# Loading queries and keys by head pair instead of by row tile, moving the first values to another queue, and building the sine tables later, in a fused attention and gated-convolution kernel

## The chip, the cores and the metric

The kernel runs on one core of a Trainium2 chip. The metric is the device time of one execution in microseconds (us). A "span" is the length of the profiled execution; it is some 2 us shorter than the device time of the same run. A run is called slow when its time is more than 1.5% above the fastest of the same kernel, and only fast runs enter a comparison. The share of full speed that the throttle granted to the matrix engine is called the granted clock.

Five engines appear in the profile: PE (matmuls; PEld is its weight load), ACT (activations, copies), DVE (vector work), POOL and SP (here mostly issuers of transfers). A line such as L381 is a line of the kernel concerned, so the same work has another line number in the kernel before (L376) and after (L381).

## The reference, cut to what matters

```python
# q, k, v: (4 batches, 8 heads, 768 positions, 64), float32
scores = q @ k.T / 8 - slope[h] * distance, kept for the 8 global keys
         and for the 96 positions up to the query; softmax; @ v
x = attention output as (4, 768, 512)
x1, x2, x3 = split(x @ w_proj, 3)              # w_proj: (512, 1536)
conv = irfft(rfft(x2) * rfft(filter_fft))      # along the 768 positions
out  = (x1 * conv * x3) @ w_out                # float32
```

The kernel does the Fourier transforms as matmuls with sine tables, in four batches. A batch passes through: load q and k (float32 in memory, float16 on the chip), transpose them, scores, exps, masks, values, transpose x, projection ("proj"), forward transform, products, inverse transform, gates, output ("out").

Of the kernel before, what the change touches and what calls it, by code (L numbers as in the profile page):

```python
# [9 lines left out]
F32 = mybir.dt.float32  # L10
# [5 lines left out]
P = 128  # L16
# [44 lines left out]
class Plan:  # L61
# [55 lines left out]
    def schedule(self):  # L117
# [27 lines left out]
        dma = [2.0]  # L145
# [4 lines left out]
        while live:  # L150
# [25 lines left out]
            if o.bytes:  # L176
                n, size = o.bytes
                dma[0] = max(dma[0], o.end + 1.8) + n * size / (306e3 if size < 512 else 390e3)
                ready = o.landed = dma[0] + 0.3
# [98 lines left out]
class Fused:  # L278
# [26 lines left out]
    def buffers(self):  # L305
# [5 lines left out]
        self.qn = t("qn", [P, 6, H, D])  # L311
        self.kn = t("kn", [P, 7, H, D])
# [23 lines left out]
        self.ot = [t(f"ot{i}", [P, DM], F32) for i in range(6)]  # L336
# [3 lines left out]
        self.dm = t("dm", [P, 3, 216], F32)  # L340
        self.dg = t("dg", [P, 216], F32)
# [37 lines left out]
    def load_rows(self, what, dst, src, b, t):  # L379

        lo, hi = max(0, self.K0[t] - NG), self.K0[t] + KL  # L381
        self.load("G", dst[P - (hi - lo):P, t, :, 0:self.D],
                  src[b, :, lo:hi, :].rearrange("h p d -> p h d"), [what + (t,)], (8 * (hi - lo), 256),
                  f"load{what}{t}")

    def load_q(self, b, t):
        src = self.q[b, :, P * t:P * t + P, :].rearrange("h p d -> p h d")
        if b == 0:
            st = self.ot[t].rearrange("p (h d) -> p h d", h=self.H)
            self.load("S", st, src, [("ot", t)], (1024, 256), f"q{t}")  # L390
            self.g.op("V", dve(512, 2), lambda e: self.copy(e, self.qn[:, t], st),
                      r=[("ot", t)], w=[("qn", t)], name="cast")
        else:
            self.load("G", self.qn[:, t], src, [("qn", t)], (1024, 256), f"q{t}")

    def load_v(self, b, ts):
        vt, s = self.vn[b % 2], b % 2
        if b < 2 and ts[0] == 0:
            self.g.op("V", 0.2, lambda _: self.nc.vector.memset(vt[:, :, :, self.D:], 1.0),
                      w=[("vn1", s)], name="ones")  # L400
        for t in ts:
            self.load_rows(("vn", s), vt, self.v, b, t)
            if t == 0:
                self.load_global(vt, s, 0, 1)
            elif t == ts[-1]:
                lo = max(1, ts[0])
                self.load_global(vt, s, lo, t + 1 - lo)
# [6 lines left out]
    def load_w(self, o, n):  # L414
        wr = self.w_proj.rearrange("(t p) n -> p t n", p=P)
        self.load("G", self.w[:, :, o:o + n], wr[:, :, o:o + n],
                  [("w", i) for i in range(o // P, (o + n) // P)], (512, 4 * n), f"w{o}")


    def setup(self):  # L420
# [4 lines left out]
        g.op("A", 0.2, lambda _: nc.scalar.activation(self.warm, self.warm, Act.Sin),  # L425
             r=["warm"], w=["warm"], table="sin", bias=-4000)
# [13 lines left out]
        g.op("V", 0.08, lambda _: v.memset(self.kn[0:NG, 0], 0.0), w=[("kn", 0)], bias=-4000)  # L440
# [9 lines left out]
    def tables(self):  # L450

        nc, g, S = self.nc, self.g, self.S
        nf = 2.0 * math.pi / S * (1.0 - 4.0e-7)
        for a in range(5):
            b = g.bank()
            g.op("P", 0.8 if a < 3 else 0.5, lambda _, a=a, b=b: self.angles(a, b.f32()),
                 r=["rows"], acq=[b], bias=-3000, name="angles")
# [4 lines left out]
                w=[("th", a)], bias=-3000)  # L462
            g.op("V", dve(n, 2), lambda _, th=th: nc.vector.tensor_scalar(
                th, th, MAGIC, -float(S), op0=Alu.subtract, op1=Alu.mult), r=[("th", a)],
                w=[("th", a)], bias=-3000)
            g.op("V", dve(n), lambda _, th=th, b=b, n=n: nc.vector.tensor_add(
                th, th, b.f32()[:, 0:n]), use=[b], r=[("th", a)], w=[("th", a)], bias=-3000)
            part = range(0, 2) if a == 3 else range(2, 3)

            def sines(_, a=a, th=th, part=part):  # L470
                if a < 3:
                    o = self.fwd[:, a, 0:4].rearrange("p s r -> p (s r)")
                else:
# [5 lines left out]
                 [("fwd", t, s) for t in part for s in (4, 5)], table="sin", bias=-3000,  # L479
                 name="sines")  # L480
# [34 lines left out]
    def distances(self):  # L515
# [4 lines left out]
        p, v, dm, dg = nc.gpsimd, nc.vector, self.dm, self.dg  # L520

        def first(_):
            for ap, w, base in ((dg, n, NG), (dm[:, 2, n - 48:n], 48, NG + o)):
# [7 lines left out]
            p.affine_select(dm[:, 2, n - 48:n], dm[:, 2, n - 48:n], pattern=[[0, 48]],  # L531
                            base=-NG - o, channel_multiplier=1, compare_op=Alu.is_ge, fill=HUGE)
        g.op("G", 1.8, first, w=["dm"], bias=-2000.0 + 5)

        def second(_):
            v.tensor_copy(dm[:, 0:2], dg[:, None, :].to_broadcast([P, 2, n]))
            v.tensor_copy(dm[:, 2, 0:n - 48], dg[:, 0:n - 48])
            v.memset(dm[0:NG, :, 0:KL], float(NL))
            v.memset(dm[0:NG, :, KL:n], HUGE)
            v.memset(dm[0:NG, 2, n - 48:n], float(NL))  # L540
            v.memset(dm[0:NG, 0, 0:KL], HUGE)
        g.op("V", 1.6, second, r=["dm"], w=["dm"], bias=-100)

        def third(_):
            d0 = dm[0:NG, 0, 0:KL]
            for sgn, off in ((1, 0), (-1, NL - 1)):
                p.affine_select(d0, d0, pattern=[[sgn, KL]], base=off, channel_multiplier=-sgn,
                                compare_op=Alu.is_ge, fill=float(NL))
        g.op("G", 0.65, third, r=["dm"], w=["dm"], bias=-2000.0 + 5)
        for h in range(self.H):  # L550
            g.op("A", act(648), lambda _, h=h: nc.scalar.activation(
                self.mask[:, h], dm.rearrange("p a b -> p (a b)"), Act.Exp, scale=-self.slopes[h]),
                r=["dm"], w=[("mask", h)], table="exp", name="mask",
                after=[x for x in g.ops if x.name == "sines"])
# [46 lines left out]
    def transposes(self, what, t, src, cols):  # L601

        nc, g = self.nc, self.g
        b = g.bank()

        def turn(_):
            for i in range(4):
                nc.tensor.transpose(b.f16()[:, P * i:P * i + P],  # L608
                                    src[:, 2 * i:2 * i + 2, :], self.ident)
        g.op("P", pe(*[128] * 4), turn, acq=[b], r=["ident", (what + "n", t)], name=what)  # L610
        lo = NG if what == "k" else 0
        dst = self.QT[:, :, cols:cols + P] if what == "q" else self.KT[:, :, cols + lo:cols + P]
        g.op("AV", {"A": act(512), "V": dve(512, 2, True)}, lambda e: self.copy(
            e, dst, b.f16()[:, 0:512].rearrange("p (i c) -> p i c", i=4)[:, :, lo:]), use=[b],
            w=[(what.upper() + "T", t)], name=what + "T")
        if what == "k" and t == 0:
            kv = self.KT.rearrange("p i (t c) -> p i t c", t=7)
            g.op("V", dve(224), lambda _: self.copy(
                "V", kv[:, :, :, 0:NG], kv[:, :, 0:1, NG:2 * NG].to_broadcast([P, 4, 7, NG])),
                r=[("KT", 0)], w=["KTg"])  # L620

    def scores(self, hp, gi):
# [15 lines left out]
        qt = range(KL * m0[0] // P, (KL * m0[-1] + self.EW[m0[-1]] - 1) // P + 1)  # L638
        g.op("P", 0.34, run, acq=bs, r=[("QT", t) for t in qt] + [("KT", m) for m in m0] + ["KTg"],
# [4 lines left out]
        for hh in range(2):  # L644
            g.op("A", act(432), lambda _, hh=hh: nc.scalar.activation(  # L645
                eo[:, hh], bs[hh].f32()[:, 0:432].rearrange("p (m w) -> p m w", m=2), Act.Exp,
                scale=self.scale), use=[bs[hh]], w=[("E", hp, gi, hh)], table="exp", name="exp")
        mk = self.mask[:, 2 * hp:2 * hp + 2].rearrange("p h (m w) -> p h m w", m=3)

        def masked(_):  # L650
# [4 lines left out]
            else:  # L655
                nc.vector.tensor_mul(eo, eo, mk[:, :, 0:2] if gi == 0 else mk[:, :, 1:3])  # L656
        g.op("V", dve(864, 2) + (0.068 if gi == 1 else 0), masked,
             r=[("E", hp, gi, 0), ("E", hp, gi, 1), ("mask", 2 * hp), ("mask", 2 * hp + 1)],
# [42 lines left out]
    def transpose_x(self, j, c):  # L701
# [5 lines left out]
        def run(_):  # L707
# [10 lines left out]
            w=[("xT", j, c)], name="xT")  # L718

    def butterfly(self, j):  # L720
        g, h, hs = self.g, self.S // 2, slice(2 * j, 2 * j + 2)
        xT = self.xT
        rs = [("xT", j, c) for c in range(3)]
# [5 lines left out]
    def gate(self, b, j, s):  # L729
        nc, g, h = self.nc, self.g, self.S // 2  # L730
        gt = self.gt[b % 2]
        xs = [("xT", i, c) for i in range(2) for c in ((0, 1) if s == 0 else (1, 2))]
# [18 lines left out]
    def attention(self, b):  # L751
        self.g.batch = (self.PERIOD * (b - 1 + self.SHIFT), self.PERIOD * self.LONG)
        for c in range(3):
            new = ([0, 1, 2], [3, 4], [5])[c]
            for t in new:
                self.transposes("q", t, self.qn[:, t], P * t)
            for t in self.GRP[c]:
                self.transposes("k", t, self.kn[:, t], P * t)
# [133 lines left out]
    def load_first(self):  # L892
        for c in range(3):
            for t in ([0, 1, 2], [3, 4], [5])[c]:
                self.load_q(0, t)
            for t in self.GRP[c]:
                self.load_rows(("kn",), self.kn, self.k, 0, t)
            if c == 0:
                self.distances()
            self.load_v(0, self.GRP[c])  # L900
        wr = self.w_proj.rearrange("(t p) n -> p t n", p=P)
        for o in (0, 256):
            self.load_w(o, 256)
            self.load_w(2 * self.DM + o, 256)
        self.load_w(self.DM, self.DM)
        self.load("G", self.fl, self.filt.rearrange("(t p) n -> p t n", p=P),
                  [("g", 1, j, s) for j in range(4) for s in range(2)], (768, 2048), "filter")

    def load_batch(self, b):
        for t in range(6):  # L910
            self.load_q(b, t)
        for t in range(7):
            self.load_rows(("kn",), self.kn, self.k, b, t)
        self.load_v(b, range(7))

    def graph(self):
# [3 lines left out]
        self.tables()  # L920
        self.load_first()
        self.attention(0)
        g.batch = (0.0, self.PERIOD / 2)
# [53 lines left out]
```

## The kernel before: what the change and the argument touch

The kernel lists its operations with their cost, their reads (`r=`) and their writes (`w=`). A list scheduler then orders them greedily for each engine by estimated times and by a priority that grows with the batch. What it puts out is a fixed order for each engine. Two facts matter later. First, `r=` and `w=` are names inside the scheduler; the waits that the chip carries out are derived from the tiles that the instructions really touch. Second, the scheduler estimates when a transfer lands.

```python
# scheduler: one line of transfers for the whole chip
n, size = o.bytes
dma[0] = max(dma[0], o.end + 1.8) + n * size / (306e3 if size < 512 else 390e3)
ready = o.landed = dma[0] + 0.3
...
key = lambda o: o.batch[0] + o.batch[1] * o.tail / (total[o.batch] or 1.0) + o.bias
# batch 0's loads; load_q(0, t): SP, float32, then a cast; else POOL, which casts on the way
def load_first(self):
    for c in range(3):
        for t in ([0, 1, 2], [3, 4], [5])[c]:
            self.load_q(0, t)                       # 128 positions, 8 heads, rows of 256 bytes
        for t in self.GRP[c]:
            self.load_rows(("kn",), self.kn, self.k, 0, t)
        if c == 0:
            self.distances()                        # masks
        self.load_v(0, self.GRP[c])                 # values, on POOL as well
    ...                                             # then the weights and the filter, on POOL
# a transpose: four 128x128 blocks (head pairs) of one row tile t into one bank, one copy out
nc.tensor.transpose(b.f16()[:, P * i:P * i + P], src[:, 2 * i:2 * i + 2, :], self.ident)
# attention of a batch: chunk by chunk, only the tiles that a chunk needs
self.g.batch = (self.PERIOD * (b - 1 + self.SHIFT), self.PERIOD * self.LONG)   # SHIFT 0, LONG 0.8
for c in range(3):
    for t in ([0, 1, 2], [3, 4], [5])[c]:
        self.transposes("q", t, self.qn[:, t], P * t)
    for t in self.GRP[c]:                            # (0,1), (2,3), (4,5,6)
        self.transposes("k", t, self.kn[:, t], P * t)
    for i in range(4):
        self.scores(i, c)
    ...                                              # values, transpose x, gates
# graph: the sine tables come first, with the highest priority (bias -3000)
self.setup(); self.tables(); self.load_first(); self.attention(0)
```

The softmax here doesn't subtract the row's maximum and nothing guards it: scores larger than these inputs give would overflow.

## Time and profile before

| | before |
|---|---|
| time, median of 3 runs (lowest to highest) | 199.46 us (199.36 to 200.19) |
| span of the profiled run | 198.0 us |
| PE busy | 185.1 us, 93% |
| transfers' packets | 90,933 |
| exps of batch 0, start of the first to start of the last | 20.9 to 32.2 us |
| first output matmul of batch 0, 1, 2; last one of all | 90.9, 128.3, 165.8; 193.7 us |

The page of the kernel before, its first part (busy us, share of the span, instructions) and the lines of its second part for PE and its clock, in 40 slices of 5 us, in tenths:

```profile
PE 185.1 (93%) x1654; PEld 109.7 (55%) x1654; DVE 151.0 (76%) x380; ACT 150.3 (76%) x305; POOL 75.7 (38%) x96
...
PE   7993699989999699999999999999999999999992
...
PEclk9998599999999969999999999999999999999999
```

PE is the engine to watch: it is nearly always busy from 40 us on. It is short of work at 15 to 25 us, and the clock falls to 0.5 there. The queues of the same page (packets, MB, share of the time of 16 DMA engines), and the summary of the chain that ended last:

```profile
q0 software_dynamic: 80912, 12.52, 95.7%
q1 hardware_dynamic: 10000, 8.10, 12.6%
...
PE 72%; DMA 10%; POOL 9%; DVE 4%; issue 2%; ACT 1%; POOLq 0%; ACTq 0%
```

POOL's queue is q0, SP's is q1. The opening, from the chain in order of time (start us, us, what):

```profile
22.84 9.44 DMA w<-in_moe_w_proj_dram
...
32.57 9.87 DMA kn<-in_k_dram
...
43.53 5.20 PE bank L739 x32
```

The program waits for projection weights until 32.3 us and for batch 1's keys until 42.4 us. ACT's timeline of the opening shows the table loaded again, the masks, and the first exps:

```profile
14.54 1.28 ACT L551 ACT_TABLE_LOAD   x1
15.83 5.17 ACT L551 ACTIVATE mask<-dm 128x648 f16<-128x648 f32 x8
20.91 6.80 ACT L645 ACTIVATE E<-bank 128x432 f16<-128x432 f32 x16
```

Two lines of the windows view. Its columns are the window and its length, then busy us and instructions of PE, PEld, DVE, ACT, POOL, then the granted clock, the DMA share, and GB/s:

```profile
20.00:25.00 5.00, 3.54 (x40) 2.66 (x39) 3.07 (x9) 5.00 (x12) 5.00 (x7) 0.50 1.79 153
...
100.00:120.00 20.00, 20.00 (x219) 12.27 (x216) 18.70 (x49) 16.46 (x35) 0.88 (x1) 1.00 0.13 17
```

At 20 to 25 us ACT is full and PE is not. At 100 to 120 us PE is full, DVE has 1.3 us left and ACT 3.5.

### The profile page before, as it was taken

Reading aid. Unit: us, or ns where it says so; the run is one execution under the profiler, and the core shown is the slowest. Engines: PE = TensorE matmul, PEld = TensorE weight load, DVE = VectorE, ACT = ScalarE, POOL = GpSimd, SP = SyncE. Lnnn points to the kernel's source line nnn. Section 1 sums busy time; section 2 is a strip of 40 time slices with the busy share of each in tenths; the row PEclk is TensorE's granted clock in tenths of the full one; section 3 lists DMA queues with packets and bytes.
Section 4 is the critical chain, followed back from the end, with each engine's and each line's share of the span. In section 5 each row is a group of like instructions: output and inputs, shape, how many; then the busy total and the mean of one; then the engine's idle time right before and its main releaser. Section 6 shows DMA issues by size and latency. Waiting matters only on the chain.

```text
span 198.0 us, 4444 instructions
## 1 busy us (share of the span) xinstructions
PE 185.1 (93%) x1654; PEld 109.7 (55%) x1654; DVE 151.0 (76%) x380; ACT 150.3 (76%) x305; POOL 75.7 (38%) x96
## 2 busy tenths in 40 slices
PE   7993699989999699999999999999999999999992
PEld 2571465755545486665455657654656665445640
DVE  5993599795599999898169999951998999159540
ACT  3889997384899987387698966857999975785852
POOL 8969983499889899085000100000000000000000
PEclk9998599999999969999999999999999999999999
DMA  7999999999999999999620400025000000214025
GB/s 156 214 152 96 152 184 209 158 157 144 147 167 156 154 154 161 108 69 148 223 110 0 30 0 0 5 106 212 3 2 3 0 3 0 106 53 159 3 108 211
DMA packets 90933, 20.90 MB, mean 106 GB/s; under 512 B 83776, under 2 KB 87840, under 8 KB 90912
## 3 DMA queue, kind: packets, MB, share of 16 engines
q0 software_dynamic: 80912, 12.52, 95.7%
q1 hardware_dynamic: 10000, 8.10, 12.6%
q8 instruction: 13, 0.21, 0.4%
q14 instruction: 8, 0.07, 0.1%
HBM read 26.61 MB, written 6.29 MB: 166 GB/s over the span
## 4 chain that ended last, share of the span: by engine, by line
PE 72%; DMA 10%; POOL 9%; DVE 4%; issue 2%; ACT 1%; POOLq 0%; ACTq 0%
PE bank L739 19%; PE bank L786 11%; PE bank L826 10%; PE bank L595 8%; PE bank L806 8%; DMA kn<-in_k_dram 5%; DMA w<-in_moe_w_proj_dram 5%; PE bank L633 4%; PE bank L677 3%; POOL vn L376 3%; PE bank L608 3%; PE bank L712 3%; POOL kn L376 3%; PE bank L682 2%; POOL w L376 1%
## 5 line engine op out<-in xcount | busy, mean ns | idle before, releaser
L739 PE MATMUL bank<-xT,w 128*128 128x384 f16 x256 | 44.1, 326 | 0.1
L645 ACT ACTIVATE E<-bank 128x432 f16<-128x432 f32 x96 | 42.7, 570 | 0.5 <-PE bank L633 0.3
L376 POOL DMA_DIRECT2D kn<-in_k_dram x28 | 25.2, 915 | 23.5 <-PE bank L608 17.8
L739 PEld LDWEIGHTS <-w 128*128 128x128 f16 x256 | 24.8, 98 | 16.9
L376 POOL DMA_DIRECT2D vn<-in_v_dram x28 | 25.2, 922 | 6.4 <-PE bank L682 5.2
L364 ACT ACTIVATE x<-bank 128x384 f16<-128x384 f32 x31 | 15.7, 508 | 15.4 <-PE bank L739 14.3
L656 DVE TENSOR_TENSOR E<-E,mask 128x864 f16<-128x864 f16 x32 | 18.6, 602 | 7.6 <-ACT E L645 7.3
L697 DVE TENSOR_TENSOR xn<-bank,rc 128x256 f16<-128x256 f32 (+1 forms) x48 | 22.5, 469 | 1.7
L826 PE MATMUL bank<-wo,y 128*128 128x512 f16 x96 | 22.4, 379 | 0.0
L747 DVE TENSOR_TENSOR g<-bank,x 128x384 f16<-128x384 f32 x32 | 17.3, 552 | 5.6 <-PE bank L739 5.2
L364 ACT ACTIVATE ot<-bank 128x512 f32<-128x512 f32 x24 | 14.3, 597 | 8.8 <-PE bank L826 8.8
L360 ACT CAST eo<-bank 128x384 f16<-128x384 f32 x31 | 14.7, 487 | 7.2 <-PE bank L806 6.8
L677 PE MATMUL bank<-vn,E 128*128 128x65 f16 x224 | 19.6, 201 | 0.1
L677 PEld LDWEIGHTS <-E 128*128 128x128 f16 x224 | 16.3, 103 | 4.9 <-DVE E L656 1.3
L682 PE MATMUL bank<-vn,E 128*128 128x65 f16 x192 | 19.1, 199 | 0.0
L806 PE MATMUL bank<-inv,X 128*128 128x384 f16 x96 | 18.7, 326 | 0.0
L595 PE MATMUL bank<-ab,fwd 128*128 128x512 f16 x72 | 18.3, 379 | 0.0
L376 POOL DMA_DIRECT2D qn<-in_q_dram x18 | 16.0, 913 | 2.2 <-PE bank L633 0.7
L633 PE MATMUL bank<-QT,KT 64*128 64x216 f16 (+2 forms) x224 | 15.9, 248 | 0.7 <-DVE inv L360 0.2
L608 PE MATMUL bank<-ident,kn 128*128 128x128 f16 x112 | 10.9, 231 | 5.8 <-ACT E L645 4.4
L682 PEld LDWEIGHTS <-E 128*128 128x128 f16 x192 | 14.7, 101 | 1.2
L826 PEld LDWEIGHTS <-y 128*128 128x128 f16 x96 | 9.4, 98 | 10.5
(103 smaller groups left out, 323.3 us busy)
## 6 DMA issues: line engine op xcount, KB each, us to landing
out_dram<-ot SPq DMA_DIRECT2D x24, 256.0 KB
kn<-in_k_dram POOLq DMA_DIRECT2D x24, 128.0 KB, 5.7
vn<-in_v_dram POOLq DMA_DIRECT2D x24, 128.0 KB, 6.2
qn<-in_q_dram POOLq DMA_DIRECT2D x18, 128.0 KB, 7.8
ot<-in_q_dram SPq DMA_DIRECT2D x6, 256.0 KB
w<-in_moe_w_proj_dram POOLq DMA_DIRECT2D x4, 256.0 KB, 6.5
g<-in_moe_filter_fft_dram POOLq DMA_DIRECT2D x1, 768.0 KB, 12.9
w<-in_moe_w_proj_dram POOLq DMA_DIRECT2D x1, 512.0 KB, 9.4
```

What stands on the lines that cost most here:

```text
L364: self.nc.scalar.mul(out, in_, c)
L376: return self.g.op(eng, 0.57 + 0.00035 * nbytes[0] if eng == "G" else 0.5, lambda _: e.dma_start(dst, src), w=w, r=r, nbytes=nbytes, name= ...
L595: self.nc.tensor.matmul(b.f32(), self.fwd[:, kt, s, :], src[i][:, kt, :], start=(kt == 0), stop=(kt == 2))
L633: nc.tensor.matmul(bs[hh].f32()[:, off:off + w], self.KT[hs, hp, P * m:P * m + P], self.QT[hs, hp, KL * m:KL * m + w], start=(off == 0), s ...
L645: g.op("A", act(432), lambda _, hh=hh: nc.scalar.activation(eo[:, hh], bs[hh].f32()[:, 0:432].rearrange("p (m w) -> p m w", m=2), Act.Exp, ...
L677: nc.tensor.matmul(o[:, hh, i], ef[:, at:at + P], vt[:, t, 2 * hp + hh, :], start=first, stop=(t == 0), skip_group_check=True)
L682: nc.tensor.matmul(o[:, hh, i], ef[:, at:at + P], vt[:, t - 1, 2 * hp + hh, :], start=False, stop=True, skip_group_check=True)
L697: nc.vector.tensor_mul(xn[:, ts[0]:ts[0] + nt].rearrange("p t h d -> p h t d"), o[:, :, :, 0:D], r.to_broadcast([P, 2, nt, D]))
L739: nc.tensor.matmul(bk.f32()[:, 0:h], self.w[:, c, o + P * j:o + P * j + P], self.xT[:, c, h * s:h * s + h], start=(c == 0), stop=(c == 3))
L786: nc.tensor.matmul(bk.f32(), src[:, c, P * t:P * t + P], w[:, c, DM:2 * DM], start=(c == 0), stop=(c == 3))
L806: nc.tensor.matmul(bk.f32()[:, 0:h], X[:, s, cs], self.inv[:, s, :], start=(s == slots[0]), stop=(s == slots[-1]))
L826: nc.tensor.matmul(bk.f32(), y[:, c, P * t:P * t + P], self.wo[:, c, :], start=(c == 0), stop=(c == 3))
```

## The change

The intent: positions are assigned to partitions six by six, so that one transfer brings a head pair in rows of 1536 bytes instead of 256. The first exps no longer stand behind the sines. The core of the diff, with cuts marked:

```diff
-        dma = [2.0]
+        dma = {"S": 2.0, "G": 2.0}                      # scheduler: two queues, a price for each packet
...
-                dma[0] = max(dma[0], o.end + 1.8) + n * size / (306e3 if size < 512 else 390e3)
+                cost = 0.012 + 3.6e-5 * size if e == "S" else 0.018 + 3.5e-5 * size
+                other = dma["SG".replace(e, "")]
+                at, work = max(dma[e], o.end + 1.8), n * cost / 16
+                both = min(max(0.0, other - at), 2.0 * work)
+                dma[e] = at + work + both / 2.0
...
+    def load_pair(self, what, b, hp):
+        hs = slice(2 * hp, 2 * hp + 2)
+        src = (self.q if what == "q" else self.k)[b, hs].rearrange("h (p t) d -> p h (t d)", t=6)
...
         nf = 2.0 * math.pi / S * (1.0 - 4.0e-7)          # tables(): no bias -3000 any more
...
+                 name="sines", after=exps)               # sines behind batch 0's exps
...                                                      # masks: a 216-wide and a 48-wide exp a head, DVE copies the rest
-                nc.tensor.transpose(b.f16()[:, P * i:P * i + P],
-                                    src[:, 2 * i:2 * i + 2, :], self.ident)
+                for hh in range(2):                      # a head pair: 12 half-width transposes a bank
+                    nc.tensor.transpose(o[64 * hh:64 * hh + 64],
+                                        src[:, 2 * hp + hh, D * t:D * t + D], self.ident)
...
     def attention(self, b):
+        for hp in range(4):
+            self.transposes("q", hp)
+            self.transposes("k", hp)
         for c in range(3):                               # no transposes in this loop any more
...
+        self.first_v()                                   # batch 0's values: SP, float32, then a cast
+        for o in (0, 2 * self.DM, self.DM):
+            self.load_w(o, self.DM, [("vn", 0, 2)])      # "reads" value tile 2
         self.load("G", self.fl, ...,
+                  [("vn", 0, 5)])                        # "reads" value tile 5
...
+    def first_v(self):
...
+            for rows, n, src in ((slice(0, NG), NG, 0), (slice(NG, P), KL, self.K0[t])):
+                self.load("S", st[rows], self.v[0, :, src:src + n].rearrange("h p d -> p h d"),
+                          [("vst", t, n)], (8 * n, 256), f"v{t}")
+            g.op("AV", ..., copy st to vt[:, t], r=[("vst", t, NG), ("vst", t, KL)] + ks, w=[("vn", 0, t)], name="vcast")
```

Batch 0's values have moved from POOL's queue, where they followed q and k, to SP's queue: 14 transfers of 256-byte rows.

## The prediction

> **What bounds the kernel now.** The page gives PE 185.1 us busy of 198.0 (93%), but 8.0 of that is filler (the idle-tile matmuls, counted start to start in the trace). Useful PE work is about 177 us. From about 42.5 us on PE is nearly solid; the loss lies before. By 42.5 us only some 29 us of useful PE work is done. The chain of waits reads in order: POOL issuing loads (0.9 us each) to 22.8 us, the DMA of the projection weights until 32.3, the DMA of batch 1's keys until 42.4, then PE. Two sub-causes in the timelines: ACT builds sines (4.6 to 11 us), reloads its table (14.5), builds masks (15.8 to 20.9), so the first exp starts at 20.9 though scores are ready at 15; DVE idles 5.2 us behind it, PE 4.4 us, and the clock falls to 0.50 (windows view, 20 to 25 us). A second loss: 64 to 72 us, PE idle 1.3 us, clock 0.69, with DVE and ACT both above 95% busy.
>
> **What the change does.** (a) Queries and keys go from 52 transfers of 256-byte rows to 32 of 1536-byte rows. Trace: 128-byte written packets (256 read) flow at 1200 per us, 307 GB/s read; 1024-byte ones (2048 read) at 200 per us, 410 GB/s. So a batch's queries and keys fall from about 11 to 8 us of DMA, and POOL issues 8 loads, not 13. (b) First values move to SP, staged in float32 and cast: seven casts, near 0.4 us each, 2.8 us of ACT or DVE. (c) First exps no longer wait for sines: I expect the first near 7 to 9 us, the 24 (10.3 us) over near 22 instead of 32.8. Cost: one more table load, 1.28 us. (d) Masks: 16 short activations instead of 8 of 728 ns (about -1.6 us), DVE spreading about +1.6 net. (e) Transposes: 96 half-width ones a batch instead of 52. The Trainium skill, "TensorE: Matmul & The Clock Gate", Part 3, says matmuls in different column groups run concurrently. Score matmuls, paired in row groups, agree here (12 of 216 columns in 0.68 us), but no trace yet shows column pairs. I expect no net change; if pairs serialize, +2 us a batch. (f) Evacuations read PSUM with a stride: 768 columns at DVE's single rate, 0.87 us against 0.40 per 512; about +2.5 us of ACT plus DVE a batch.
>
> **On the critical path.** DMA: I estimate weights landed near 25 us (was 32.3), filter near 29 (36.5), batch 1's queries and keys near 38 (42.4). That alone would give 5 to 9 us. But ACT plus DVE are busy some 129 of 160 us in the first 80 us, and the change adds about 7 there; they will allow 4 to 6 us. After 80 us I expect nothing, PE stays solid. Predicted 194.0 us, range 188.5 to 199.5; chances: faster 0.6, same 0.36, slower 0.04.
>
> **Signs.** Right: first exp before 10 us; no throttled slice at 20 to 25 us; weights landed by 27 us; PE solid from about 36 us; DMA slices empty earlier. Wrong: transposes above 60 ns a pair-member start to start; exps late because copies crowd ACT; PE stalls after 40 us behind DVE.
>
> **What would break it.** ACT and DVE turning the opening into a longer stall (time same); PE column pairs serializing (up to +7 us); SP's 14 value transfers landing late and holding back weights, which wait for them; or, the other way, better overlap that reaches the PE floor, about 177 + 5 at start + 4 at the tail = 186 us.

## The result, and the profile after

| | before | after |
|---|---|---|
| time, median of 4 runs each, same rounds | 199.82 us (199.36 to 200.52) | 227.67 us (227.23 to 227.81) |
| span of the profiled run | 198.0 | 225.9 |
| transfers' packets | 90,933 | 44,464 |
| exps of batch 0, first start to last start | 20.9 to 32.2 | 21.6 to 56.1 |
| first output matmul of batch 0, 1, 2; last one | 90.9, 128.3, 165.8; 193.7 | 113.6, 155.2, 194.1; 222.0 |

The change costs 28 us. The ratio is 1.1386, with a 95% interval of 1.1343 to 1.1429. A ratio here is the mean time of one kernel's fast runs over that of the other's of the same rounds, so it is not quite the ratio of the medians that are quoted. All runs gave correct results.

The last row divides the loss: 22.7 us of it exist when batch 0's first output is computed. From there to batch 1's first output the kernel after takes 41.6 us where the kernel before takes 37.4, to batch 2's 38.9 against 37.5, and to the end 27.9 in both. So the loss is 22.7 + 4.2 + 1.4 us. The two parts have different causes.

The page of the kernel after, the same lines:

```profile
PE 187.5 (83%) x1821; PEld 108.7 (48%) x1821; DVE 153.3 (68%) x396; ACT 155.7 (69%) x324; POOL 46.5 (21%) x69
...
PE   7742003248999999989999999999999999999993
...
PEclk9995555556999999999999999999999999999999
...
q0 software_dynamic: 32352, 11.12, 44.5%
q1 hardware_dynamic: 12089, 9.88, 16.1%
...
PE 53%; SPq 17%; ACT 14%; DVE 7%; DMA 4%; issue 2%; DVEq 0%; ACTq 0%
...
h<-in_v_dram SPq DMA_DIRECT2D x6, 240.0 KB, 17.2
```

The packets have halved, POOL has 29 us less to do, and PE works for a quarter of the time between 20 and 50 us (7.5 us of 30, by the windows view), at half the clock. SP's sequencer (SPq) has become 17% of the chain; and one of SP's transfers of values (`h<-in_v_dram`, the last line) takes 17.2 us from issue to landing in the median. The chain in order of time:

```profile
15.94 6.49 SPq L381
...
23.28 6.32 SPq L381
...
40.21 9.88 DMA X<-in_v_dram
```

SP needs up to 6.49 us to issue one of them. In e10 below, where values flow freely, its 14 issues are over at 21 us instead of 42, so these issues seem to wait for room behind the transfers before them; the trace names no such wait. The timelines of SP, and of POOL meanwhile:

```profile
2.77 33.17 SPq L381 DMA_DIRECT2D h<-in_v_dram  x12
35.99 5.65 SPq L381 DMA_DIRECT2D X<-in_v_dram  x2
```

```profile
7.08 0.97 POOL L381 DMA_DIRECT2D wo<-in_moe_w_out_dram  x1
...
8.81 2.38 POOL L381 DMA_DIRECT2D w<-in_moe_w_proj_dram  x3
11.17 0.85 POOL L381 DMA_DIRECT2D g<-in_moe_filter_fft_dram  x1
11.98 0.90 POOL L381 DMA_DIRECT2D qn<-in_q_dram  x1
```

POOL issues all weights at 8.81 us, although `load_w` "reads" value tile 2, which is written at 33 us. The name in `r=` only placed the transfer in the order. No instruction of the transfer touches the value tile, so nothing waits. What waits for values is the cast, in the queues of ACT and DVE. From the waits view of the kernel after (us in total, times, longest):

```profile
DVE vn L365 <- DMA h<-in_v_dram: 22.6, 4, 9.1
...
ACT vn L365 <- DMA h<-in_v_dram: 13.4, 2, 10.1
```

And ACT's timeline, where the exps of batch 0 stand behind such a cast:

```profile
21.59 1.01 ACT L676 ACTIVATE E<-bank 128x432 f16<-128x432 f32 x2
...
47.39 0.62 ACT L365 CAST vn<-h 128x512 f16<-128x512 f32 x1 [10.12 <-DMA h<-in_v_dram]
```

The Trainium skill, "PSUM — Partial Sum Buffer", section "Engine vs sequencer instructions", says that ScalarE's and VectorE's queues are strict FIFO. This trace agrees: ACT was idle for 10.12 us at the head of that line, and six exps followed at once. Two windows of the kernel after:

```profile
20.00:25.00 5.00, 1.12 (x10) 0.28 (x6) 0.00 (x0) 2.61 (x7) 0.88 (x2) 0.50 1.22 197
...
40.00:50.00 10.00, 3.69 (x35) 2.44 (x36) 3.14 (x10) 2.61 (x7) 3.00 (x4) 0.50 1.82 155
```

Why do values come so slowly? I counted the packets in the trace in steps of 2 us, by queue and by the bytes that a packet writes (a weight packet that writes 1024 bytes reads 2048):

```
kernel after          POOL's queue (q0)              SP's queue (q1), values of 256 bytes
14 to 16 us           311 of 1024 bytes              285
18 to 20 us           309 of 1024 bytes              295
22 to 24 us           312 of 1024 bytes              289
34 to 36 us           357 of 768 bytes (q and k)     361
44 to 46 us           1725 of 128 bytes (values)     270
```

From 10 to 40 us about as many packets pass on one queue as on the other, as if they took turns, packet for packet. For each packet POOL's queue then moves 2048 bytes from memory, or 1536, and SP's moves 256. Beside the weights, values get some 145 packets a microsecond, and the last of them land near 50 us. From 42 us on, where POOL's queue has narrow rows too, the counts are no longer equal (the last line); why is open. The Trainium skill, "DMA: Bandwidth & Descriptors", section "Queues, rings and completion order", says that each DMA engine round-robins between queue rows at packet granularity. The counts to 40 us agree with the taking of turns. They do not show its grain: the page's packet holds several descriptors (9 to 17 are typical, it says), a packet of the profile is one row, and the trace does not tell which of the 16 engines moved it.

So the first theory is: **values starve behind wide packets of the other queue (theory of the queues)**, and in-order engines pass their wait on. Rivals: SP's path for 256-byte rows is slow by itself; the float32 staging with casts costs it; the scheduler's new transfer prices give a bad order; the moved sines do.

### The profile page after: what moved, and what is told of

The parts are those of the page before. It is cut to its first block, busy times and chain, and to the rows that moved or that the text cites. A ratio compares the mean times of both kernels' runs of the same rounds, so it can differ in the third digit from the quotient of the medians.

```text
span 225.9 us, 4780 instructions
## 1 busy us (share of the span) xinstructions
PE 187.5 (83%) x1821; PEld 108.7 (48%) x1821; DVE 153.3 (68%) x396; ACT 155.7 (69%) x324; POOL 46.5 (21%) x69
## 2 busy tenths in 40 slices
DMA packets 44464, 21.30 MB, mean 94 GB/s; under 512 B 30193, under 2 KB 41369, under 8 KB 44441
## 4 chain that ended last, share of the span: by engine, by line
PE 53%; SPq 17%; ACT 14%; DVE 7%; DMA 4%; issue 2%; DVEq 0%; ACTq 0%
PE bank L771 18%; SPq L381 17%; PE bank L856 9%; ACT E L676 7%; PE bank L836 7%; PE bank L816 5%; DMA X<-in_v_dram 4%; PE bank L615 4%; PE bank L631 3%; ACT ab L365 2%; DVE E L685 2%; PE bank L709 2%; PE bank L744 2%; ACT X L365 2%; ACT h L369 1%
## 5 line engine op out<-in xcount | busy, mean ns | idle before, releaser
L676 ACT ACTIVATE E<-bank 128x432 f16<-128x432 f32 x96 | 44.9, 578 | 12.5 <-PE bank L665 12.3
L771 PE MATMUL bank<-xT,w 128*128 128x384 f16 x256 | 44.2, 326 | 0.6 <-ACT h L369 0.6
L771 PEld LDWEIGHTS <-w 128*128 128x128 f16 x256 | 24.6, 98 | 17.4 <-issue 0.8
L665 PE MATMUL bank<-QT,KT 64*128 64x216 f16 (+2 forms) x224 | 18.8, 265 | 14.3 <-DVE y L477 6.8
L709 PE MATMUL bank<-vn,E 128*128 128x65 f16 x224 | 19.1, 200 | 9.7 <-DVE E L688 8.0
L381 POOL DMA_DIRECT2D vn<-in_v_dram x21 | 18.7, 894 | 36.0 <-PE bank L714 21.8
L709 PEld LDWEIGHTS <-E 128*128 128x128 f16 x224 | 15.7, 101 | 16.3 <-DVE E L688 11.5
L688 DVE TENSOR_TENSOR E<-E,mask 128x864 f16<-128x864 f16 x32 | 18.7, 602 | 3.5 <-ACT E L676 3.4
L665 PEld LDWEIGHTS <-KT 64*128 64x128 f16 x224 | 9.2, 98 | 24.0 <-DVE KT L365 11.4
L714 PE MATMUL bank<-vn,E 128*128 128x65 f16 x192 | 18.6, 198 | 0.0
L836 PE MATMUL bank<-inv,X 128*128 128x384 f16 x96 | 18.1, 326 | 0.0
L365 DVE CAST vn<-h 128x512 f16<-128x512 f32 x4 | 2.3, 565 | 22.6 <-DMA h<-in_v_dram 22.6
L381 POOL DMA_DIRECT2D kn<-in_k_dram x16 | 11.6, 724 | 21.5 <-PE bank L631 10.9
L365 ACT CAST ab<-bank 128x512 f16<-128x512 f32 x22 | 13.0, 614 | 3.8 <-PE bank L816 3.7
L714 PEld LDWEIGHTS <-E 128*128 128x128 f16 x192 | 14.6, 101 | 1.0 <-issue 0.3
## 6 DMA issues: line engine op xcount, KB each, us to landing
h<-in_v_dram SPq DMA_DIRECT2D x6, 240.0 KB, 17.2
```

The source lines that it names most:

```text
L365: {"A": nc.scalar.copy, "V": nc.vector.tensor_copy, "G": nc.gpsimd.tensor_copy}[e](out, in_)
L381: return self.g.op(eng, 0.57 + 0.00035 * nbytes[0] if eng == "G" else 0.5, lambda _: e.dma_start(dst, src), w=w, r=r, nbytes=nbytes, name= ...
L665: nc.tensor.matmul(bs[hh].f32()[:, off:off + w], self.KT[hs, hp, P * m:P * m + P], self.QT[hs, hp, KL * m:KL * m + w], start=(off == 0), s ...
L676: g.op("A", act(432), lambda _, hh=hh: nc.scalar.activation(eo[:, hh], bs[hh].f32()[:, 0:432].rearrange("p (m w) -> p m w", m=2), Act.Exp, ...
L709: nc.tensor.matmul(o[:, hh, i], ef[:, at:at + P], vt[:, t, 2 * hp + hh, :], start=first, stop=(t == 0), skip_group_check=True)
L714: nc.tensor.matmul(o[:, hh, i], ef[:, at:at + P], vt[:, t - 1, 2 * hp + hh, :], start=False, stop=True, skip_group_check=True)
```

## The experiments

All 17 kernels gave correct results. "Ratio" is to the kernel before in the same rounds. Kernels of one call shared the runs of the kernel before, whose median was 199.65 to 200.49 us in the calls.

### Cause 1: values behind wide packets

**e1_v_pool.** Values go back to POOL's queue, in front of the weights, with the cast on the way.

```diff
-        self.first_v()
+        self.load_v(0, range(7))
```

> The changed kernel, but batch 0's values go through POOL's queue as before, ahead of the weights (seven loads, no staging, no casts). Theory A (values starve on SP's queue, because the weights, filter and batch 1's loads on POOL's queue are not held back and take most of the engines' time): values landed by about 22 us instead of 46, PE solid from about 35 to 40 us, 190 to 198 us in all. Rival C (the new transposes, strided evacuations or sines placed late cause the loss): above 215 us.

Measured: 208.98 us (207.97 to 209.43), ratio 1.0454. This takes back 18.7 of 28 us, and lies between the two ranges that were expected. It can't tell the queue from the staging, so the next one is needed.

**e2_hold.** The change as it is, with the wait made real: before each transfer that "reads" a value tile, POOL copies one element of that tile.

```diff
+    def hold(self, r):
+        if r and r[0][:2] == ("vn", 0):
+            self.nc.gpsimd.tensor_copy(self.held[:, 0:1], self.vn[0][0:1, r[0][2], 0, 0:1])
```

> The changed kernel with the same order on PE, ACT, DVE and SP; on POOL each load that the plan holds for a value cast really waits, by a copy of one element out of that value tile. Theory A: with no other queue active the values move at 900 packets per us or more instead of about 145, the last one lands before 22 us, and the time falls to 191 to 200 us although the weights are issued later (about 15 us instead of 9). Rival B (SP's loads of 120 and 8 partitions with 256-byte rows are slow by themselves): the rate stays near 145 to 200 per us, values still land after 40 us, weights later still, over 235 us.

Measured: 206.05, 206.46 and 206.88 us in the three fast runs, ratio 1.0321. A fourth run fell in a slow state (274 us), and its profile with it, so the profile of e2 isn't used. The order on PE, ACT, DVE and SP is that of the kernel after, instruction by instruction; only POOL's copies are added. So 21 of 28 us go when nothing is done but to keep wide packets out of the way of the values. Theory A wanted 191 to 200 us: it names the larger part of the loss and not all of it. The staging, the casts and SP's queue are all still there: those rivals fall.

The twin of e2, e10 (below), shows SP and POOL in their timelines:

```profile
2.77 17.17 SPq L381 DMA_DIRECT2D h<-in_v_dram  x12
19.98 1.21 SPq L381 DMA_DIRECT2D X<-in_v_dram  x2
```

```profile
20.64 0.18 POOL L992 COPY held<-vn 1x1 f16<-1x1 f16 x1 [11.78 <-DVE vn L365]
20.76 0.76 POOL L381 DMA_DIRECT2D w<-in_moe_w_proj_dram  x1
```

SP is through with its issues at 21 us instead of 42. The counts of packets in e10:

```
e10_hold_fit          POOL's queue (q0)              SP's queue (q1), values of 256 bytes
12 to 14 us           210 of 1024 (wo), 121 of 768   329
14 to 16 us           244 of 1024 (wo), 6 of 768     489
16 to 18 us            48 of 1024 bytes             1513
18 to 20 us             0                           1462
20 to 22 us             0                           1661
```

The same transfers run at 145 packets a microsecond beside wide packets and at 730 to 830 alone. (The last row landed at 27.3 us, not by the 23 that were expected.)

**e3_told.** The starving is left; the scheduler is told when values really land (17.8 to 50.1 us), so that it places casts late. The false reads are dropped.

```diff
-                ready = o.landed = dma[e] + 0.3
+                ready = o.landed = max(dma[e] + 0.3, LANDED.get(o.name, 0.0))
```

> The changed kernel, same transfers; only the plan is told when the values really landed (17.8 to 50.1 us) and that weights are not held, so it queues the value casts late on ACT and DVE instead of ahead of key copies and exps. Values land as late as before. Theory A with a second link (in-order ACT and DVE stuck behind a cast that waits): the 24 exps end before 32 us instead of 56, and the time falls by 8 to 18 us, to 209 to 220. Rival (only the late values as such matter, not the queue order): within 3 us of 227.

Measured: 215.27 us, ratio 1.0751. Batch 0's exps ran at 18.7 to 28.2 us, and batch 0's first output came at 99.8 us instead of 113.6. So another order alone takes back 12 of the 28 us, and in its waits view no cast of ACT or DVE waits for values any more. That the blocked queues cost all of the 12 isn't shown apart, for POOL's queue was ordered anew as well: the output weights (`wo`) went from 7.08 to 42.75 us, behind the projection weights. Values that come late cost some 9 us more (215.3 against 206.5 in e2) even in an order that expects them late.

**e4_narrow_w.** Each weight load is cut into four of 128 columns, so that its packets write 256 bytes, at the same place of the order.

```diff
-lambda _: e.dma_start(dst, src)
+lambda _: [e.dma_start(dst[:, :, i:i + P], src[:, :, i:i + P]) for i in range(0, 512, P)] if name in ("w0", "w512", "w1024") else ...
```

> The changed kernel, same order on every engine; each weight load split in four of 128 columns, so that its packets carry 512 bytes of float32 instead of 2048. Theory A says that the two queues take turns packet by packet: then the values' rate beside the weights rises from about 145 packets per us to 300 or more, with about as many weight packets. Rival (queues share by bytes, or the values' rate is SP's own limit): the values' rate stays between 120 and 180 per us.

Measured: one run, 221.48 us (state unknown for a single run; its span was 219.6 against 225.9). The counts answer the question that the run was made for: from 24 to 30 us there are 660 to 709 weight packets beside 611 to 628 value packets in 2 us. Not every step is so even: at 18 to 20 us it is 869 to 449, at 22 to 24 us 996 to 325, and why is open. Over 18 to 30 us the values come at some 270 a microsecond, about twice as fast as beside wide packets, and at 310 in the even steps. So the same values move faster when only the neighbour's packets are made narrower. That rules out a limit of SP's own, and it shows that the width of the neighbour's packets counts; an exact one for one is not shown.

### The scheduler's price

**e5_pool_fit.** e1, with the scheduler's price for 256-byte packets on POOL's queue set to what the trace of the kernel before shows (1200 a microsecond on 16 engines, 13.3 ns for each engine; the change charged 27 ns), and with 10 ns less for every wider packet there.

```diff
-  0.018 + 3.5e-5 * size
+  (0.0133 if size == 256 else 0.008 + 3.5e-5 * size)
```

> The run with batch 0's values through POOL, and the plan's price for a packet on POOL's queue set to what the traces show (13.3 ns per engine at 256 bytes, 43.7 at 1024, 80 at 2048, instead of 27, 54 and 90). Theory D (the second half of the loss, 209 against 199.7, is queue order: the plan believes batch 2's queries and keys land at 72 to 82 us, where they land by about 58, and queues their transposes and scores late): 197 to 202 us, the period from one batch's first output matmul to the next falls from 43.1 to below 40 us. Rival E (transposing by head pair needs all of the previous batch's scores of that pair, which by itself bunches the exps): stays at 205 to 209.

Measured: 206.06 us (205.6 to 206.53), ratio 1.0316. It is 3 us better than e1 and still 3% behind, in rival E's range and not in theory D's. The price alone doesn't explain what is left.

**e7_before_newmodel.** The kernel before with nothing but the change's lines for the price of a transfer.

> The kernel before, with the change's DMA prices alone (the plan's two lines), no other edit: same transfers, same instructions, another order. Theory D: slower by 2 to 6 per cent, 203 to 212 us. Rival (the prices hardly matter): within 1 per cent of 199.7.

Measured: 215.01 us, ratio 1.0765, above the expected 203 to 212. The price can cost 15 us on a kernel whose loads it misjudges: there nearly all q, k and v rows are 256 bytes on POOL's queue.

**e10_hold_fit.** e2 with the corrected price.

> The changed kernel with both mends and values still on SP's queue: weights and later loads on POOL's queue really wait for the value casts, and the plan prices POOL's packets as measured. If the two causes (starved values, prices) are all that separates it from the run through POOL with measured prices: 203 to 208 us, within 3 us of that run's 206, and the values land by 23 us at 700 or more packets per us.

Measured: 206.0, 207.59 and 208.0 us in the three fast runs (a fourth, slow, took 210.09), ratio 1.0347 with an interval of 1.026 to 1.0434. That is e2 again, within the noise. So with the values mended on SP's queue the price makes no difference that can be seen, while with values on POOL's queue it was worth 3 us (e1 against e5). e2 and e5 mend the values in different ways and meet at 206 us.

### Cause 2: the last 6 us

The rest isn't in the opening. Stages of the kernels that follow, from the traces (us; starts of the first output matmul of batch 0, 1, 2, of the last one of all, and of the first and last exp of batch 2):

| kernel | batch 0 | batch 1 | batch 2 | last | exps of batch 2 |
|---|---|---|---|---|---|
| before | 90.9 | 128.3 | 165.8 | 193.7 | 85.5 to 119.0 |
| after | 113.6 | 155.2 | 194.1 | 222.0 | 124.6 to 140.5 |
| e5 | 90.9 | 132.8 | 171.7 | 199.6 | 102.2 to 118.1 |
| e11 | 93.4 | 133.1 | 170.6 | 198.5 | 90.7 to 123.5 |
| e16 | 90.8 | 133.2 | 169.0 | 196.9 | 102.1 to 123.7 |
| e12 | 88.9 | 130.6 | 167.3 | 195.0 | 97.8 to 121.8 |
| e17 | 89.0 | 130.6 | 166.7 | 194.6 | 97.9 to 121.9 |
| e14 (before, sines late) | 93.3 | 130.7 | 168.2 | 196.1 | 87.9 to 121.4 |
| e15 (before, transposes ahead) | 91.8 | 129.2 | 167.8 | 195.6 | 88.6 to 115.4 |
| e18 (before, priorities spread) | 88.6 | 127.9 | 166.0 | 195.2 | 86.4 to 121.5 |

e5 has batch 0's first output at the same time as the kernel before and loses 4.5 us by batch 1's and 1.4 by batch 2's, as the kernel after does (4.2 and 1.4). The exps of batch 2 are packed into 16 us instead of 34. The chain of e5 at that place, and its window:

```profile
102.62 3.06 ACT E L676 x7
...
107.02 0.97 ACT ab L365 x2
...
116.21 5.31 PE bank L771 x32
```

```profile
100.00:120.00 20.00, 19.82 (x234) 11.62 (x231) 17.82 (x48) 19.11 (x42) 1.40 (x2) 1.00 0.21 46
```

ACT is busy for 19.11 us of 20 and is the chain from 102.6 to 112.5 us; in the kernel before it is busy for 16.46 and the chain there is PE throughout. That suggests that ACT sets the pace; e11 below tests it. The gates (L771) begin at 116.2 instead of 112.3 us. PE is called busy in both (19.82 and 20.00 us): the busy share does not show that it works at another engine's pace.

**e8_tables_first.** e5 with the sine tables at the front again, masks behind them, as in the kernel before.

> The run with values through POOL and measured prices, and the sine tables put back to the front (the change's last part undone). If moving the sines behind batch 0's exps is worth what I predicted, this is 1 to 4 us slower than the run with the sines behind. The rival: the front is bound by the queries and keys that land until 11 us, so ACT has the time for the sines anyway, and the move only adds a table load: 1 to 3 us faster.

Measured: 204.35 us, ratio 1.0222, 0.8% below e5. That is what the rival said: with the sines at the front the kernel is a little faster.

**e9_scores_early.** e8, with a pair's first scores directly behind its transposes in the list (and left out of the later loop).

```diff
             self.transposes("k", hp)
+            self.scores(hp, 0)
```

> The last one, and in the attention stage the first group's scores of a head pair are planned right after its transposes instead of after all eight. Theory E as a smaller second term: exps of later batches start earlier and spread out, 1 to 3 us off. If it all holds, 193 to 197 us, below the kernel before.

Measured: 202.07 us, ratio 1.0108, above the 193 to 197 that were expected.

**e11_spread, e12_spread_early, e13_spread_early_first.** e11 is e5 with the attention's priorities spread over the whole period; e12 adds e9's early scores; e13 adds e8's early sines.

```diff
-    SHIFT = 0.0
-    LONG = 0.8
+    SHIFT = -0.1
+    LONG = 1.0
```

> Values through POOL, measured prices, and only the plan's two stage numbers changed (attention starts 4 us earlier in priority and is stretched over a whole period instead of 0.8 of it), so that the plan spreads batch 2's exps over 34 us instead of 16. Theory E' (what is left of the loss, 206 against 200, is that the exps of batches 2 and 3 come bunched beside the projection and spectrum stage and ACT ends every wait there): 200 to 203 us; ACT below 90 per cent busy in the projection and spectrum stage; first output to first output of batches 1 and 2 below 40 us, from 41.9. If ACT's bunching is not the cause: 205 to 207.

> The same, and the first group's scores of a head pair planned right after its transposes. Theory E': another 1 to 3 us, 197 to 201 us, about the kernel before or just under.

> The same with the sine tables at the front. If the 0.8 per cent that the sines at the front gained in the earlier pair holds here: 196 to 200 us; if that gain was only an accident of the order, 1 to 2 us slower than the run before.

Measured: e11 204.08 us, ratio 1.0191; e12 201.29, ratio 1.005 (0.9978 to 1.0122); e13 201.23, ratio 1.005. Order alone takes back 5 of the 6 us: the work is the same, though the scheduler also hands some copies from ACT to DVE or back (of the 24 projection copies `ab`, ACT has all in e5 and 19 in e12). With a good order the place of the sines makes no difference (e12 against e13).

Whether ACT's packed exps cost the first 4.5 us, e11 leaves open. Its windows:

```profile
80.00:100.00 20.00, 19.19 (x233) 12.23 (x228) 17.43 (x42) 18.79 (x41) 8.05 (x11) 1.00 1.08 132
100.00:120.00 20.00, 19.77 (x181) 10.90 (x180) 15.23 (x42) 15.60 (x32) 0.00 (x0) 1.00 0.15 57
```

At 100 to 120 us ACT is busy for 15.60 of 20 us instead of 19.11, batch 2's exps are spread over 33 us, and the stretch from batch 0's to batch 1's first output falls from 41.9 to 39.6 us, as theory E' wanted. But now ACT is full at 80 to 100 us (18.79), and batch 0's first output comes 2.5 us later, so batch 1's is no earlier than in e5 (133.1 and 132.8): the load was moved. The 204.08 us miss the expected 200 to 203, and what e11 gains comes after that point. e12 has the early scores too and is at 130.6 there. So the order is the cause, and which part of it holds batch 1 back is open.

**e14_before_sines.** The other way round: the kernel before with nothing but the change's sines, distances and masks.

> The kernel before, with its loads and its transposes by row tile, and only the change's last part: sines behind batch 0's exps, masks built earlier and spread. First exp near 13 us instead of 20.9. If the start is bound by ACT's and DVE's total work, as my prediction had as its limit, the earlier exps buy little: first output matmul at 89 to 92 us as before (90.9), 198 to 201 us. If the sines in front were the bound: 194 to 197 us.

Measured: 202.86 us (202.46 to 203.59), ratio 1.014, above both ranges. Batch 0's exps start at 16.3 instead of 20.9 us, and projection starts at 44.6 instead of 48.6; then a stall gives all of it back. The window of e14 where it does:

```profile
60.00:80.00 20.00, 15.61 (x187) 11.69 (x186) 16.53 (x42) 15.40 (x32) 17.64 (x20) 0.83 2.50 149
```

PE is busy for 15.61 us of 20, where the kernel before has 18.40. The first output comes at 93.3 us, later than before. What ends the stall I did not test.

**e15_before_all_first.** The kernel before, with all 13 transposes of a batch ahead of its scores in the list, as the change has its eight.

> The kernel before, with the same loads and transposes by row tile, only the plan's list for the attention stage has all 13 transposes ahead of the first scores, as the change has its eight. If the bunching of exps comes from this order: exps of batches 1 and 2 bunch and the time rises by 3 to 7 us, to 203 to 207. If it comes from transposing by head pair (all rows of a pair, so that nothing of the next batch can start before the last scores of that pair): within 2 us of 199.7.

Measured: 201.3 us, ratio 1.0052 (0.9999 to 1.0105). The order of the list is worth half a per cent on the kernel before (1% at the upper end of the interval). The packing of exps isn't its doing alone.

These 14 kernels left this open: is the packing forced by buffers, since a pair's transposed q and k can't be overwritten before all scores of that pair of the batch before are done, or by priorities?

**e16_double.** e5 with two buffers of transposed q and k, by parity of the batch.

```diff
+        self.QT, self.KT, self.par = self.QTs[b % 2], self.KTs[b % 2], b % 2
```

> e5 with two buffers of transposed queries and keys, by parity of the batch, nothing else. Theory B (the bunching comes from the pair-wide single buffers, which keep batch b+1's transposes behind all of batch b's scores of that pair): exps of batch 2 start by 92 us instead of 102, batch 1's first output by 130 us, 201 to 203 us in all. Rival S (the bunching comes from the order that the scheduler's priorities give, the buffers don't bind): batch 2's exps still start near 102, 204.5 to 206.5 us.

Measured: 202.89 us (202.66 to 202.98), ratio 1.0128 (1.0068 to 1.0189). Neither side was right. The time falls by 3 us, as theory B wanted, but not where it wanted: batch 2's exps still start at 102.1 us. The gain is in the next batch, whose exps start at 131.1 instead of 143.7 us, so that the stretch from batch 1's to batch 2's first output falls from 38.9 to 35.8 us. So the buffers bind batch 3, in this order. Batch 2 is packed by the order: it took e11's priorities to start its exps at 90.7 us.

**e17_double_spread.** e12 with these buffers.

> e12 (priorities spread, scores of a pair directly behind its transposes, values on the other queue) with the two buffers of e16. Theory B: 1 to 3 us below e12's 201.3, so 198.5 to 200.5, the first version below the kernel before. Rival S: 201 to 202, like e12.

Measured: 200.06 us (199.87 to 200.63), ratio 0.9995 (0.9944 to 1.0047). It lies within theory B's range, but the step from e12 (1.005 to 0.9995) is smaller than the intervals are wide, so what the second buffer adds to e12 isn't clear of noise. The chain of e17 in the stretch that ACT held in e5, and its window:

```profile
98.91 0.97 PE bank L819 x4
...
107.61 1.73 PE bank L819 x8
...
114.77 5.31 PE bank L771 x32
```

```profile
100.00:120.00 20.00, 20.00 (x221) 11.62 (x218) 18.64 (x47) 18.21 (x39) 0.00 (x0) 1.00 0.07 28
```

The chain is PE again, and PE's busy time is 20.00 of 20.

**e18_before_spread.** The control: e11's priorities on the kernel before.

> The kernel before with nothing but e11's priorities (start of a batch 4 us earlier, spread over the whole period). If the priorities merely repair what the change bunched, the kernel before gains nothing: 199 to 201 us. If they are a gain of their own, it falls by 2 to 4 us to 196 to 198, and then e12's parity hides a loss of the change of the same size.

Measured: 201.28 us, ratio 1.0061 (1.0007 to 1.0115). The kernel before gains nothing from them. So what they recover in e11 and e12 is damage that the change did to the order, not a gain that the kernel before could have had too. (Its batch 0 has its first output at 88.6 us, though, as early as in e12.)

No version was faster than the kernel before. The best form of the change, e17, equals it within half a per cent.

## Why the prediction was wrong, point by point

Predicted were 194.0 us, within 188.5 to 199.5. Measured were 227.67 us. The direction was wrong.

**The step that failed.** In the prediction's words: "(b) First values move to SP, staged in float32 and cast", costed as "2.8 us of ACT or DVE"; and, among the risks, "SP's 14 value transfers landing late and holding back weights, which wait for them". I costed the casts and not the transfers' company, and I read `r=[("vn", 0, 2)]` as a wait of the chip. It was only a place in the order. The runs showed the reverse: weights went out at 8.81 us and held back the values, which landed near 50 us (e2: making that wait real takes 21 us off). The rates that I used for transfers, 200 to 1200 packets a microsecond, are rates of a queue that is alone. The Trainium skill, "DMA: Bandwidth & Descriptors", section "Issuing engines are not separate DMA queues", says that transfers of all issuers run on the same 16 engines and interleave. The counts here agree, with about one packet each up to 40 us, and that is the term that the sum lacked.

**The DMA terms on POOL's side were right for the weights alone.** I estimated weights landed near 25 us, the filter near 29, batch 1's q and k near 38. Adding up the packets of the kernel after, the weights' last one passed near 26 us, the filter's near 32, and q's and k's near 43, later than in the kernel before (42.4). And the weights' time was bought from the values. (The change also loads `wo`, the output weights, ahead of the projection weights, at 7.08 us, where the kernel before issues them at 48.8 us. Only e3 took that back, among other things.) The sign "weights landed by 27 us" came true in a kernel that was 28 us slower: it watched the wrong transfers.

**"That alone would give 5 to 9 us ... they will allow 4 to 6."** With the values mended and the order good (e12) batch 0's first output comes at 88.9 us instead of 90.9. An opening that is better by 2 us is the best that was seen, and it is gone by batch 1's first output (130.6 against 128.3). Even these 2 us can't be put down to the earlier weights (landed at 29.1 us in e12, at 32.3 before): the kernel before reaches 88.6 us with e11's priorities alone (e18).

**First exps "near 7 to 9 us".** They started at 21.6 us in the kernel after, at 17.7 in e5 and at 13.0 in e12. The direction holds when the values are mended, the size does not: mask exps (3.2 us in a row) and copies out of the transposes stand before them on ACT. And the point is worth nothing: e14, which moves the sines and changes the masks and nothing else, is 1.4% slower than the kernel before.

**Transposes: right.** "I expect no net change." The chain of the kernel before and that of the kernel after show a bank or two of them (start, us, how many):

```profile
52.81 0.45 PE bank L608 x8
```

```profile
64.01 0.46 PE bank L631 x12
```

Twelve half-width ones take 0.46 us with the end of the last, eight whole ones 0.45. Counted from start to start in rows at the full clock, whole ones follow each other after 56 ns; of the half-width ones the second of a pair starts 3 to 4 ns after the first, and a pair follows a pair after 56 ns, so 28 ns each. A batch has 96 of them, 2.7 us, or 52 whole ones, 2.9 us. The pairs do run side by side, as the Trainium skill, "TensorE: Matmul & The Clock Gate", Part 3, says of column groups.

**Copies out of the transposes: right direction, too large.** I put "about +2.5 us of ACT plus DVE a batch". Over all four batches the copies to QT and KT take 29.3 us of ACT and DVE in the kernel before (from the groups: 12.8 + 10.2 + 2.8 + 2.7 + 0.8) and 33.6 in e5 (11.0 + 9.7 + 4.1 + 3.7 + 2.8 + 1.8 + 0.5), so 1.1 us a batch.

**"After 80 us I expect nothing, PE stays solid": wrong by 6 us.** PE did stay busy, but its share said nothing of order. In the order that the change leaves, a batch's exps are packed, ACT is the chain from 102.6 to 112.5 us in e5, and 4.5 + 1.4 us go. Spread priorities, early scores and a second buffer bring the total back (e17), and the same priorities bring nothing to the kernel before (e18). That the order is the cause is shown; that it works through ACT's packed exps is only argued: e11 spreads them, and batch 1's first output comes no earlier.

**What stays open.** In e17 the stretch from batch 0's to batch 1's first output is still 41.6 us (37.4 before); a better opening and a shorter next stretch make up for it. That the larger ACT and DVE load of the pair-wide copies causes it is only argued: between 90 and 130 us ACT is busy for 32.99 us in e17 and 30.61 before. Nor did I take away the stall at 60 to 80 us of e14, or `wo` alone from the opening, or find out why the counts of packets are uneven in some steps.

## What to carry to other kernels

When two queues are busy at once, count their packets and not their bytes: here a queue of short rows beside one of long rows got about one short packet for each long one (some 145 a microsecond instead of 730 to 830), so put the urgent transfer on the queue of the bulk one and ahead of it, or make the bulk transfer wait for real. A dependency in your own scheduler is not a wait on the chip unless an instruction touches the data. And when a change to the opening is worth little or costs more than its sum, look at the order that it leaves for later batches, because a busy PE hides which engine set the pace.

## What the Trainium skill lacked or had wrong

- "DMA: Bandwidth & Descriptors", section "Queues, rings and completion order": taking turns by packet is there, its consequence for mixed sizes is not. Here a queue of 256-byte packets got 145 a microsecond beside packets that read 2048 bytes, some 270 (310 in even steps) beside packets that write 256, and 730 to 830 alone.
- "TensorE: Matmul & The Clock Gate", Part 4: it gives a transpose's duration in a kernel as about 275 ns and no rate for transposes in a row. The groups here have a mean of 226 to 231 ns for a record of a whole one, but in a row they start 56 ns apart, and half-width ones in column pairs take 28 ns each. A budget made from the page's duration would be five to ten times too high.
- No page that I read says that a transfer which is staged in float32 puts its wait at the head of an in-order compute queue, where a transfer that casts on its way leaves it in the DMA queue. In the kernel after ACT and DVE stood 36.0 us in six such waits (13.4 + 22.6), and an order with the casts late was worth 12 us (e3, whose order differed in more than that).
